# Reordering the hand-over from filter construction to the gated MLP in a one-core S4 + SwiGLU kernel: earlier product of the first block, split additions, weights in other memory

## Chip, cores, metric

The kernel runs on one core of one Trainium2 chip. The metric is the device time of one execution in microseconds (us), the median of several. A span read in a profile runs from the first to the last instruction and is about 1.8 us shorter than the time (310.9 against 312.68 us for the profiled run before).

Engines: PE is the TensorE matmul unit, DVE is VectorE, ACT is ScalarE, POOL is GpSimd. PSUM is the memory that the matmuls here write to.

## The reference

The input x has 2048 tokens of 640 channels. Cut to what matters:

```python
K = einsum("dn,dnl,dn->dl", C, exp(dt*A*l), dt*B).real    # one filter of 2048 taps per channel
u = layernorm(x)
y = causal_fft_convolution(u, K) + u * Dskip              # the kernel does this in blocks of 256 tokens
h = x + y
h2 = h + (silu(ln(h) @ w1) * (ln(h) @ w3)) @ w2           # 640 -> 1536 -> 640
```

## The kernel before

The kernel has two halves. The first builds the filters in the frequency domain, `kf`, for three groups of channels (256, 256 and 128). `k_mm` and `k_dft` are matmuls, `k_evac` and `kf_evac` copy their results out of PSUM. The second half runs eight blocks of 256 tokens, `c` = 0 to 7. For a block, `fwd` is a Fourier transform by matmul, `product` multiplies by `kf` on DVE (block c also needs block c−1), `inv` transforms back, and `h_add` adds the result into the residual and takes its statistics. Then come `ln2_apply`, transposes, six gate/up pairs (`gu`, each ending in a product `hm` on DVE) and two groups of 24 output matmuls (`out_mm`). Four more names: `stats` and `ln1` are the statistics and the scaling of the first layer norm (`ln1` also makes `usd`, the folded input that `fwd` reads), `skip` adds `u * Dskip` into the residual, and `warm` runs matmuls whose result nobody reads, put in for the PE clock. While block c is in its matmuls, DVE and ACT prepare blocks c+1 and c+2.

This is the hand-over, shortened:

```python
    for ig, st in zip(IGS, stg):
        b_mul(2, bt2, "exp", ig, st)          # DVE, last operand for group 2
    warm(6, last_b(2, bt2, 0))
    for b in range(nb[2]):
        pk = k_mm(2, at2, bt2, kc, b)
        k_evac(2, pk, kc, b)
    for q, part in ((0, 0), (0, 1), (1, 0), (1, 1)):
        fwd(0, q, part)
    pb = k_dft(2, kc)
    stats(1); stats(2); skip(0, ulns[0]); ln1(1); skip(1, ulns[1])
    for q, part in ((0, 0), (0, 1)):
        fwd(1, q, part)
    kf_evac(2, pb, "SSVV")                    # kf is complete only here
    # ... (weight loads start, held back until kf is there)
    run(p0, 2)                                # product(0), columns 0-319, all of it behind kf
    for k in range(2): inv_mm(0, k, 0, p1[k])
    run(p0)                                   # columns 320-639
    for k in range(2): inv_mm(0, k, 1, p1[k]); y_evac(0, k, p1[k])
    for q, part in ((1, 0), (1, 1)): fwd(1, q, part)
    h_add(0); r0 = rstd(hst[0][:, :, 1], 2, V)
    # ... (ln2_apply, transposes, their eviction)
```

And the start of the loop over blocks, shortened:

```python
    for c in range(NC):
        pr = product(1) if c == 0 else iter(())
        run(pr, 2)
        for fp in range(FT // 2):             # six gate/up pairs
            gu(c, fp)                         # 10 matmuls each for gate and up, then hm on DVE
            if fp == 0: run(pr); ln1(c + 2)
            if fp in (i0, i0 + 1):
                inv(c + 1, fp - i0)
                if fp == i0 + 1: h_add(c + 1); rs = rstd(...)
            if fp >= 2: fwd(c + 2, (fp - 2) // 2, fp % 2)
            if fp == 3: stats(c + 3)
            if fp == 4 and c: pr = product(c + 2); run(pr, 2)
```

Of the kernel before, what the change touches and what calls it, by code (L numbers as in the profile page):

```python
# [16 lines left out]
II = 16  # L17
# [9 lines left out]
def kernel(  # L27
# [321 lines left out]
    def k_dft(h, kc):  # L349
# [3 lines left out]
        for i in range(II):  # L353
            for f in range(NFT):
# [58 lines left out]

    def bn(mv, k, src):
        st = small.tile([P, 2, V.BN_STATS_DIM], F32, name="st")
        for q in range(2):
            V.bn_stats(out=st[:, q, :], in_=src[:, q * (D // 2):(q + 1) * (D // 2)])  # L417
        V.bn_aggr(out=mv[:, k, :], in_=st[:])
# [30 lines left out]
    def fwd(c, q, part):  # L449
# [4 lines left out]
        pv = ps2()  # L454
# [80 lines left out]
    wts = ctx.enter_context(tc.tile_pool(name="wts", bufs=1, side="right", reuse_waits="tile"))  # L535
    w1sb = wts.tile([P, DT, F], BF16, name="w1sb")
    w3sb = wts.tile([P, DT, F], BF16, name="w3sb")
# [8 lines left out]
    kc = kp.tile([P, II * 4 * 2 * (max(CHUNKS) // 8)], BF16, name="kc")  # L546
    warm(6, last_b(2, bt2, 0))
    for b in range(nb[2]):
        pk = k_mm(2, at2, bt2, kc, b)
        k_evac(2, pk, kc, b)  # L550
    for q, part in ((0, 0), (0, 1), (1, 0), (1, 1)):
        fwd(0, q, part)
    S.activation(out=sil[:], in_=mask[:, 0:1], func=ACT.Silu)
    pb = k_dft(2, kc)
# [5 lines left out]

    def ln1(c):
        ulns[c] = ln1_apply(c, *st1.pop(c), 0)
        fold(c, ulns[c])

    stats(1)
    stats(2)
    skip(0, ulns[0])
    ln1(1)
    skip(1, ulns[1])
    for q, part in ((0, 0), (0, 1)):  # L570
        fwd(1, q, part)
    kf_evac(2, pb, "SSVV")
# [4 lines left out]
    mp = ctx.enter_context(tc.tile_pool(name="mp", bufs=1, side="left", reuse_waits="tile"))  # L577
    w2sb = mp.tile([P, FT, D], BF16, name="w2sb")
# [7 lines left out]
    zz, xx, hst, xls, xts = {}, {}, {}, {}, {}  # L586

    def product(c):


        vt = vts[c]
        t2 = mp.tile([P, 2, 2, D], BF16, name="t2", bufs=1)
        z = mp.tile([P, 2, 2, D], BF16, name="z", bufs=2)
        x = z if c == 0 else mp.tile([P, 2, 2, D], BF16, name="xf", bufs=2)
        zz[c], xx[c] = z, x
        zp = zz.pop(c - 1, None)
        kt = kr if c % 2 else kf
        n = D // 2
        for q in range(2):
            r = slice(q * n, (q + 1) * n)  # L600
            for dst, w in ((z, 0), (t2, 1)):
                kk = mkap(kt[:], w * 2 * D + q * n, [[kt[:].ap[0][0], P], [0, 2], [D, 2], [1, n]])
                V.tensor_tensor(out=dst[:, :, :, r], in0=vt[:, :, :, r], in1=kk, op=ALU.mult)  # L603
            yield
            V.tensor_tensor(out=z[:, 0, :, r], in0=z[:, 0, :, r], in1=t2[:, 1, :, r], op=ALU.subtract)
            V.tensor_tensor(out=z[:, 1, :, r], in0=z[:, 1, :, r], in1=t2[:, 0, :, r], op=ALU.add)
            if c:
                V.tensor_tensor(out=x[:, :, :, r], in0=z[:, :, :, r], in1=zp[:, :, :, r], op=(ALU.add if c % 2 else ALU.subtract))  # L608
            yield

    def inv_mm(c, k, q, py):

        for e in range(2):
            if c % 2:
                lhsT, src = (gn[:, k, :] if e == k else gt[:, 2 * k + e, :]), 1 - k
            else:
                lhsT, src = gt[:, 2 * k + e, :], k
            T.matmul(py[:, q, 0:D // 2], lhsT=lhsT, rhs=xx[c][:, src, e, q * (D // 2):(q + 1) * (D // 2)], start=(e == 0), stop=(e == 1))  # L618

    yss = {}  # L620

    def y_evac(c, k, py):
        if k == 0:
            yss[c] = mp.tile([P, 2, D], BF16, name="ys", bufs=1)
        S.copy(out=yss[c][:, k, :].rearrange("p (q d) -> p q d", q=2), in_=py[:, :, 0:D // 2])

    def h_add(c):
        ys = yss.pop(c)
        yt = mp.tile([P, 2, D], BF16, name="yt", bufs=1)
        V.tensor_tensor(out=yt[:, 0, :], in0=ys[:, 0, :], in1=ys[:, 1, :], op=ALU.add)  # L630
        V.tensor_tensor(out=yt[:, 1, :], in0=ys[:, 0, :], in1=ys[:, 1, :], op=ALU.subtract)
        V.tensor_tensor(out=xs[:, 2 * c:2 * c + 2, :], in0=yt[:], in1=xs[:, 2 * c:2 * c + 2, :], op=ALU.add)  # L632
        hst[c] = small.tile([P, 2, 2], F32, name="hmv")
        for k in range(2):
            bn(hst[c], k, xs[:, 2 * c + k, :])

# [54 lines left out]
    def inv(c, k):  # L691
        py = ps2()
        for q in range(2):
            inv_mm(c, k, q, py)
        y_evac(c, k, py)

    p0, p1 = product(0), [ps2(), ps2()]
    run(p0, 2)
    for k in range(2):
        inv_mm(0, k, 0, p1[k])  # L700
    run(p0)
    for k in range(2):
        inv_mm(0, k, 1, p1[k])
        y_evac(0, k, p1[k])
    for q, part in ((1, 0), (1, 1)):
        fwd(1, q, part)
# [6 lines left out]
    for k in range(2):  # L713
        ln2_apply(0, k, hst[0], r0, k)
        tr_mm(0, k, tp)
    for k in range(2):
        tr_evac(0, k, tp, "SV"[k])

    for c in range(NC):
# [4 lines left out]
        for fp in range(FT // 2):  # L724
            gu(c, fp)
            if fp == 0:
                run(pr)
                if n2:
                    ln1(c + 2)
# [69 lines left out]
```

## Time and profile before

| what | before |
|---|---|
| time, median | 313.11 us in the first five runs, 312.98 over 15 |
| kf complete (last eviction ends) | about 107.2 us |
| first gate matmul | 122.84 us |
| blocks 0 to 6, first gate matmul to the next block's | 27.43, 23.45, 23.06, 23.06, 23.06, 22.37, 21.27 us |

The profile's page gives each engine's busy share in 40 equal slices (a digit is tenths; 9 is 90% or more), and the clock that TensorE was granted:

```profile
PE   3152074645847443988999999999999999999994
...
DVE  6899999999999777669999789789789769462211
...
PEclk9999998576899655899999999999999999999998
```

In slices 3 to 13 DVE is full. From slice 17 on PE is full. Between them, in slices 14 to 16 (101 to 124 us), neither is, and the PE clock is down to about half (digits 6, 5, 5).

Next, the stretch view of the kernel before for that hand-over. The columns are the stretch and its length, then busy us and number of instructions of PE, PE weight loads, DVE, ACT and POOL, then granted clock, DMA share and GB/s:

```profile
94.00:108.00 14.00, 8.41 (x332) 6.10 (x332) 11.38 (x31) 8.50 (x15) 5.78 (x16) 0.84 0.02 4
108.00:118.00 10.00, 3.76 (x12) 1.45 (x12) 7.99 (x19) 5.08 (x8) 0.00 (x0) 0.50 0.97 308
118.00:123.00 5.00, 1.40 (x11) 1.19 (x12) 2.98 (x13) 0.69 (x1) 0.00 (x0) 0.50 1.08 355
```

PE works 5.2 of the 15 us from 108 to 123, at clock 0.50, and DVE leaves 4 of these 15 us empty. Neither engine is full, so this is a chain of waits, and the timeline shows its links. Its columns are start, duration, engine, line, operation, operands, shapes and count, then the idle time before it and what ended it. The DVE and PE lines of the kernel before that matter:

```profile
107.06 0.83 DVE L603 TENSOR_TENSOR z<-vt,kf 128x1280 bf16<-128x1280 bf16 x1 [1.61 <-ACT kf L370]
...
113.65 0.49 DVE L630 TENSOR_TENSOR yt<-ys 128x640 bf16<-128x640 bf16 x1 [1.70 <-ACT ys L625]
...
119.79 0.80 DVE L640 TENSOR_SCALAR xl<-xs,hmv,rs 128x640 bf16<-128x640 bf16 x2
...
122.30 0.49 DVE L654 COPY xt<-ps 128x640 bf16<-128x640 bf16 x1 [1.71 <-ACT xt L652]
...
122.84 2.29 PE L665 MATMUL ps<-xt,w1sb 128*128 128x256 bf16 x10 [1.31 <-DVE xt L654]
...
128.47 0.43 DVE L673 TENSOR_TENSOR hm<-sg,up 128x512 bf16<-128x512 bf16 x1 [2.43 <-ACT up L672]
...
133.45 0.43 PE L457 MATMUL ps<-usd,ft 128*128 128x320 bf16 x2 [0.81 <-DVE usd L446]
```

The product waits for the last `kf` eviction until 107.06, and the residual addition for the evicted inverse until 113.65. The layer norm starts at 119.79, the first gate matmul at 122.84. Even then DVE waits 2.43 us for the first gate/up result before the rest of `product(1)` and `ln1(2)`, which makes PE wait 0.81 us for block 2's folded input `usd` at 133.45.

All waits of PE after 118 us in the kernel before (who waited for whom, us in total, times, longest):

```profile
PE ps L645 <- DVE xl L640: 5.9, 1, 5.9
PE ps L679 <- DVE hm L673: 3.7, 5, 1.4
PE ps L665 <- DVE xt L654: 1.3, 1, 1.3
PE ps L457 <- DVE usd L446: 0.8, 1, 0.8
PE ps L618 <- DVE xf L608: 0.2, 1, 0.2
```

Inside the blocks the only repeated one is the output matmul on the last `hm`, five times. The timeline of block 3 shows how it arises:

```profile
200.27 0.42 DVE L673 TENSOR_TENSOR hm<-sg,up 128x512 bf16<-128x512 bf16 x1 [1.55 <-ACT up L672]
...
203.00 0.43 DVE L673 TENSOR_TENSOR hm<-sg,up 128x512 bf16<-128x512 bf16 x1 [0.66 <-ACT up L672]
...
214.99 0.42 DVE L673 TENSOR_TENSOR hm<-sg,up 128x512 bf16<-128x512 bf16 x1
...
215.47 0.72 PE L679 MATMUL ps<-w2sb,hm 128*128 128x320 bf16 x4 [0.53 <-DVE hm L673]
```

DVE has two holes early in the block (1.55 and 0.66 us, both waits for an evicted gate/up pair). The last `hm` starts at 214.99, and PE waits 0.53 us for that.

### The profile page before, as it was taken

The numbers are of one execution on the slowest core, as the hardware profiler recorded it, in microseconds if no ns is written. First come the engines' busy times: TensorE is split into PE (matmuls) and PEld (weight loads), VectorE is DVE, ScalarE is ACT, GpSimd is POOL, SyncE is SP. The second block draws the span as 40 slices with busy tenths as digits, with TensorE's granted clock in tenths as the row PEclk, the third lists the DMA queues.
The fourth block names the chain that finished last, engine by engine and source line by source line (L and its number), as shares of the span: only waits on it lengthen the run. The fifth ranks groups of instructions, "written<-read, shape, count | busy, mean of one in ns | idle before, by whom it ended". The sixth has DMA issues, their size and how long they took to land.

```text
span 310.9 us, 6842 instructions
## 1 busy us (share of the span) xinstructions
PE 234.5 (75%) x2770; PEld 185.0 (60%) x2770; DVE 246.8 (79%) x543; ACT 191.4 (62%) x389; POOL 45.2 (15%) x137
## 2 busy tenths in 40 slices
PE   3152074645847443988999999999999999999994
PEld 1121043543634212776886887887887887887882
DVE  6899999999999777669999789789789769462211
ACT  3999999999937452364465465465465465544441
POOL 4022000000003300005315015015015020020000
PEclk9999998576899655899999999999999999999998
DMA  6731910000000099200000100100100100100001
GB/s 185 211 154 34 236 36 0 2 2 3 2 3 2 7 332 354 73 2 0 24 21 0 44 2 1 44 0 3 42 2 0 44 0 2 42 2 21 24 1 43
DMA packets 12018, 15.58 MB, mean 50 GB/s; under 512 B 2002, under 2 KB 11346, under 8 KB 11858
## 3 DMA queue, kind: packets, MB, share of 16 engines
q1 hardware_dynamic: 11426, 14.95, 15.6%
q8 instruction: 21, 0.34, 0.5%
q10 hardware_dynamic: 560, 0.20, 0.3%
q14 instruction: 11, 0.09, 0.1%
HBM read 12.26 MB, written 2.88 MB: 49 GB/s over the span
## 4 chain that ended last, share of the span: by engine, by line
DVE 52%; PE 37%; ACT 6%; issue 3%; POOL 0%; DVEq 0%; POOLq 0%; ACTq 0%
PE ps L665 19%; PE ps L679 11%; DVE at L307 6%; DVE st L417 6%; DVE tt L309 6%; DVE at L312 6%; DVE bt L283 3%; DVE bt L282 3%; DVE hm L673 2%; DVE t L603 2%; DVE z L603 2%; DVE xf L608 2%; DVE xs L632 2%; PE ps L645 1%; PE ps L618 1%
## 5 line engine op out<-in xcount | busy, mean ns | idle before, releaser
L665 PE MATMUL ps<-xt,w1sb 128*128 128x256 bf16 x480 | 61.5, 276 | 1.3 <-DVE xt L654 1.3
L670 ACT ACTIVATE sg<-ps 128x512 bf16<-128x512 f32 x48 | 28.7, 597 | 54.4 <-PE ps L665 54.4
L665 PE MATMUL ps<-xt,w3sb 128*128 128x256 bf16 x480 | 61.3, 276 | 0.0
L679 PE MATMUL ps<-w2sb,hm 128*128 128x320 bf16 x384 | 55.5, 299 | 3.7 <-DVE hm L673 3.7
L665 PEld LDWEIGHTS <-w1sb 128*128 128x128 bf16 x480 | 47.6, 99 | 9.4 <-issue 1.5
L665 PEld LDWEIGHTS <-w3sb 128*128 128x128 bf16 x480 | 47.5, 99 | 5.9
L679 PEld LDWEIGHTS <-hm 128*128 128x128 bf16 x384 | 36.8, 98 | 19.1 <-DVE hm L673 5.6
L673 DVE TENSOR_TENSOR hm<-sg,up 128x512 bf16<-128x512 bf16 x48 | 19.6, 422 | 33.6 <-ACT up L672 33.6
L408 POOL TENSOR_TENSOR ta<-rs 128x2 f32<-128x2 f32 x30 | 8.6, 286 | 188.7 <-DVE rs L406 187.6
L687 ACT CAST ob<-ps 128x640 bf16<-128x640 f32 x16 | 11.1, 692 | 36.3 <-PE ps L679 36.3
L417 DVE BATCH_NORM_STATS2 st<-xs 128x6 f32<-128x320 bf16 x64 | 27.4, 471 | 2.4 <-DMA xs<-in_A_u_dram 2.1
L672 ACT CAST up<-ps 128x512 bf16<-128x512 f32 x48 | 27.8, 579 | 0.0
L325 PE MATMUL ps<-bt,at 128*128 128x128 bf16 (+1 forms) x320 | 19.9, 247 | 8.7 <-ACT kc L345 7.8
L325 PEld LDWEIGHTS <-at 128*128 128x128 bf16 (+1 forms) x320 | 17.2, 110 | 12.4 <-issue 9.3
L458 ACT CAST vt<-ps 128x640 bf16<-128x640 f32 x32 | 22.2, 706 | 3.2 <-PE ps L457 3.2
L253 ACT ACTIVATE bt<-alp 128x384 bf16<-128x384 f32 (+1 forms) x45 | 20.8, 461 | 0.0
L307 DVE TENSOR_TENSOR at<-at,zs 128x1536 bf16<-128x1536 bf16 (+3 forms) x30 | 20.3, 677 | 0.0
L309 DVE TENSOR_TENSOR tt<-at,zs 128x1536 bf16<-128x1536 bf16 (+3 forms) x30 | 20.3, 675 | 0.0
L312 DVE TENSOR_TENSOR at<-at,tt 128x1536 bf16<-128x1536 bf16 (+3 forms) x30 | 19.1, 678 | 0.5
L379 PEld LDWEIGHTS <-ident 128*128 128x128 bf16 x36 | 4.2, 123 | 22.2 <-issue 17.2
L358 PE MATMUL ps<-kc,wt 32*128 32x64 bf16 (+1 forms) x768 | 8.5, 202 | 11.7 <-ACT kc L345 6.3
L457 PE MATMUL ps<-usd,ft 128*128 128x320 bf16 x64 | 14.7, 318 | 2.5 <-ACT kc L345 1.0
(116 smaller groups left out, 379.1 us busy)
## 6 DMA issues: line engine op xcount, KB each, us to landing
xs<-in_A_u_dram SPq DMA_DIRECT2D x4, 640.0 KB, 5.1
out_dram<-ot SPq DMA_DIRECT2D x16, 160.0 KB, 1.8
wt<-ftd SPq DMA_DIRECT2D x4, 512.0 KB, 7.5
w1sb<-in_B_w_dram SPq DMA_DIRECT2D x3, 640.0 KB, 6.9
w3sb<-in_B_w_dram SPq DMA_DIRECT2D x3, 640.0 KB, 9.5
w2sb<-in_B_w_dram SPq DMA_DIRECT2D x1, 1920.0 KB, 14.5
ftd<-fl SPq DMA_DIRECT2D x1, 256.0 KB, 2.1
par_ar<-in_A_A_re_dram SPq DMA_DIRECT2D x2, 96.0 KB, 3.9
```

The source lines that it names most:

```text
L253: S.activation(out=dst, in_=grp(h, 1), func=ACT.Sin, scale=-float(i))
L307: V.tensor_tensor(out=av[:, part, :, o0:o0 + w, :], in0=src, in1=z4[:, 0].broadcast_to([P, cw // 2, w, 2]), op=ALU.mult)
L309: V.tensor_tensor(out=tv[:, part], in0=src, in1=z4[:, 1].broadcast_to([P, cw // 2, w, 2]), op=ALU.mult)
L312: V.tensor_tensor(out=dst, in0=dst, in1=tv[:, 1 - part], op=(ALU.add if part else ALU.subtract))
L325: T.matmul(pk[:, half, gi * P:(gi + 1) * P], lhsT=at[r, c], rhs=bt[r, c], start=first, stop=last, tile_position=((r.start, 0) if n1 else N ...
L417: V.bn_stats(out=st[:, q, :], in_=src[:, q * (D // 2):(q + 1) * (D // 2)])
L458: S.copy(out=vts[c][:, part, :, r], in_=pv[:, :, 0:D // 2])
L665: T.matmul(pg[:, b, u * TB:(u + 1) * TB], lhsT=w[:, kt, fb * P:(fb + 1) * P], rhs=xts[c][:, kt, :], start=(kt == 0), stop=(kt == DT - 1))
L670: S.activation(out=sg[:], in_=pg[:, 0, :], func=ACT.Silu)
L672: S.copy(out=up[:], in_=pg[:, 1, :])
L673: V.tensor_tensor(out=hms[c][:, 2 * fp:2 * fp + 2, :].rearrange("p u t -> p (u t)"), in0=sg[:], in1=up[:], op=ALU.mult)
L679: T.matmul(po[:, q, 0:D // 2], lhsT=hms[c][:, fb, k * P:(k + 1) * P], rhs=w2sb[:, fb, q * (D // 2):(q + 1) * (D // 2)], start=(fb == 0), s ...
```

## The change

The intent is to take work out of the chain behind the last `kf` eviction. Columns 0 to 511 belong to filter groups 0 and 1 and are complete long before group 2. So their product, inverse and residual addition go ahead of it, the inverse into the middle of `k_dft(2)`. Only 128 columns are left behind. For that `fwd(0)` moves ahead of `k_mm(2)`. `fwd(1)` and `skip(1)` move behind the residual addition of block 0, and the second half of `product(1)` and `ln1(2)` move ahead of block 0's first `hm`. `h_add` is split by column halves in every block. The two first weight matrices move into memory that becomes free later. The core of the diff:

```diff
-    def k_dft(h, kc):
+    def k_dft(h, kc, mid=None):
         for i in range(II):
+            if mid and i == II // 2:
+                mid()
+    HALVES = [slice(0, D // 2), slice(D // 2, D)]
+    SPLIT = [slice(0, d0s[-1]), slice(d0s[-1], D)]        # 512 and 128 columns
@@ fwd
-        pv = ps2()
+        pv = ps2("g" if c == 0 and q != part else "d")
@@ hand-over
-    warm(6, last_b(2, bt2, 0))
+    for q, part in ((0, 0), (0, 1), (1, 0), (1, 1)):
+        fwd(0, q, part)
+    skip(0, ulns[0])
+    stats(1)
+    warm(2, last_b(2, bt2, 0))
+    p0 = product(0, SPLIT)
     for b in range(nb[2]):
         pk = k_mm(2, at2, bt2, kc, b)
+        if b:
+            run(p0, 2)
         k_evac(2, pk, kc, b)
-    pb = k_dft(2, kc)
-    stats(1) ; stats(2) ; skip(0) ; ln1(1) ; skip(1) ; half of fwd(1)       (shortened)
-    kf_evac(2, pb, "SSVV")
+    pb = k_dft(2, kc, lambda: inv(0, SPLIT[0]))
+    stats(2)
+    h_add(0, SPLIT[0])
+    kf_evac(2, pb, "SSSS")
+    run(p0)
+    ln1(1)
+    inv(0, SPLIT[1])
     ... (kr)
+    warm(8, xs[:, 12:14, 0:256].rearrange("p a (b c) -> p a b c", b=1))
+    h_add(0, SPLIT[1])
+    h_stats(0)
     ... (rstd, ln2_apply, transposes)
+    skip(1, ulns[1])
     ... (eviction of the transposes)
+    for q, part in ((0, 0), (0, 1), (1, 0), (1, 1)):
+        fwd(1, q, part)
@@ loop over blocks
+            if c == 0 and fp == 0:
+                run(pr)
+                ln1(2)
             gu(c, fp)
             if fp == 0:
                 run(pr)
-                if n2:
+                if n2 and c:
                     ln1(c + 2)
             if n1 and fp in (i0, i0 + 1):
-                inv(c + 1, fp - i0)
+                inv(c + 1, HALVES[fp - i0])
+                h_add(c + 1, HALVES[fp - i0])
                 if fp == i0 + 1:
-                    h_add(c + 1)
+                    h_stats(c + 1)
```

More of the change, by code (lines that the diff above doesn't have):

```diff
@@ L412, in rstd @@
         return rs
+    HALVES = [slice(0, D // 2), slice(D // 2, D)]
+    SPLIT = [slice(0, d0s[-1]), slice(d0s[-1], D)]
     def bn(mv, k, src):
         st = small.tile([P, 2, V.BN_STATS_DIM], F32, name="st")
-        for q in range(2):
-            V.bn_stats(out=st[:, q, :], in_=src[:, q * (D // 2):(q + 1) * (D // 2)])
+        for q, r in enumerate(HALVES):
+            V.bn_stats(out=st[:, q, :], in_=src[:, r])
         V.bn_aggr(out=mv[:, k, :], in_=st[:])
@@ L534 @@
     bctx.close()
-    wts = ctx.enter_context(tc.tile_pool(name="wts", bufs=1, side="right", reuse_waits="tile"))
-    w1sb = wts.tile([P, DT, F], BF16, name="w1sb")
-    w3sb = wts.tile([P, DT, F], BF16, name="w3sb")
     vp = ctx.enter_context(tc.tile_pool(name="vp", bufs=4, side="right", reuse_waits="tile"))
@@ L545 @@
         b_mul(2, bt2, "exp", ig, st)
-    kc = kp.tile([P, II * 4 * 2 * (max(CHUNKS) // 8)], BF16, name="kc")
-    warm(6, last_b(2, bt2, 0))
-    for b in range(nb[2]):
-        pk = k_mm(2, at2, bt2, kc, b)
-        k_evac(2, pk, kc, b)
     for q, part in ((0, 0), (0, 1), (1, 0), (1, 1)):
         fwd(0, q, part)
-    S.activation(out=sil[:], in_=mask[:, 0:1], func=ACT.Silu)
-    pb = k_dft(2, kc)
     st1 = {}
@@ L559, in stats, with product @@
         st1[c] = (mv, rstd(mv[:, :, 1][:, 0:2], 2, G))
+    skip(0, ulns[0])
+    stats(1)
+    kc = kp.tile([P, II * 4 * 2 * (max(CHUNKS) // 8)], BF16, name="kc")
+    warm(2, last_b(2, bt2, 0))
+    zz, xx, hst, hpart, xls, xts = {}, {}, {}, {}, {}, {}
+    def product(c, cuts=HALVES):
+        vt = vts[c]
+        t2 = vp.tile([P, 2, 2, D], BF16, name="t2", bufs=1)
+        z = vp.tile([P, 2, 2, D], BF16, name="z", bufs=2)
+        x = z if c == 0 else vp.tile([P, 2, 2, D], BF16, name="xf", bufs=2)
+        zz[c], xx[c] = z, x
+        zp = zz.pop(c - 1, None)
+        kt = kr if c % 2 else kf
+        for r in cuts:
+            for dst, w in ((z, 0), (t2, 1)):
+                kk = mkap(kt[:], w * 2 * D + r.start, [[kt[:].ap[0][0], P], [0, 2], [D, 2], [1, r.stop - r.start]])
+                V.tensor_tensor(out=dst[:, :, :, r], in0=vt[:, :, :, r], in1=kk, op=ALU.mult)
+            yield
+            V.tensor_tensor(out=z[:, 0, :, r], in0=z[:, 0, :, r], in1=t2[:, 1, :, r], op=ALU.subtract)
+            V.tensor_tensor(out=z[:, 1, :, r], in0=z[:, 1, :, r], in1=t2[:, 0, :, r], op=ALU.add)
+            if c:
+                V.tensor_tensor(out=x[:, :, :, r], in0=z[:, :, :, r], in1=zp[:, :, :, r], op=(ALU.add if c % 2 else ALU.subtract))
+            yield
@@ new lines, with inv @@
+    yss = {}
+    def inv(c, r):
+        py, n = ps2(), r.stop - r.start
+        for k in range(2):
+            for e in range(2):
+                if c % 2:
+                    lhsT, src = (gn[:, k, :] if e == k else gt[:, 2 * k + e, :]), 1 - k
+                else:
+                    lhsT, src = gt[:, 2 * k + e, :], k
+                T.matmul(py[:, k, 0:n], lhsT=lhsT, rhs=xx[c][:, src, e, r], start=(e == 0), stop=(e == 1))
+        if r.start == 0:
+            yss[c] = vp.tile([P, 2, D], BF16, name="ys", bufs=1)
+        S.copy(out=yss[c][:, :, r], in_=py[:, :, 0:n])
@@ new lines, in h_add @@
+    def h_add(c, r):
+        ys = yss[c]
+        if r.start == 0:
+            hpart[c] = vp.tile([P, 2, D], BF16, name="yt", bufs=1), small.tile([P, 2, 2, V.BN_STATS_DIM], F32, name="hst")
+        yt, st = hpart[c]
+        V.tensor_tensor(out=yt[:, 0, r], in0=ys[:, 0, r], in1=ys[:, 1, r], op=ALU.add)
+        V.tensor_tensor(out=yt[:, 1, r], in0=ys[:, 0, r], in1=ys[:, 1, r], op=ALU.subtract)
+        V.tensor_tensor(out=xs[:, 2 * c:2 * c + 2, r], in0=yt[:, :, r], in1=xs[:, 2 * c:2 * c + 2, r], op=ALU.add)
+        for k in range(2):
+            V.bn_stats(out=st[:, k, int(r.start > 0), :], in_=xs[:, 2 * c + k, r])
@@ L561, in ln1, with h_stats @@
+    def h_stats(c):
+        hst[c] = small.tile([P, 2, 2], F32, name="hmv")
+        for k in range(2):
+            V.bn_aggr(out=hst[c][:, k, :], in_=hpart[c][1][:, k])
     def ln1(c):
@@ L563, in ln1 @@
         fold(c, ulns[c])
-    stats(1)
-    stats(2)
-    skip(0, ulns[0])
-    ln1(1)
-    skip(1, ulns[1])
-    for q, part in ((0, 0), (0, 1)):
-        fwd(1, q, part)
-    kf_evac(2, pb, "SSVV")
+    p0 = product(0, SPLIT)
+    for b in range(nb[2]):
+        pk = k_mm(2, at2, bt2, kc, b)
+        if b:
+            run(p0, 2)
+        k_evac(2, pk, kc, b)
+    S.activation(out=sil[:], in_=mask[:, 0:1], func=ACT.Silu)
+    pb = k_dft(2, kc, lambda: inv(0, SPLIT[0]))
+    stats(2)
+    h_add(0, SPLIT[0])
+    kf_evac(2, pb, "SSSS")
     kctx.close()
@@ L577 @@
     mp = ctx.enter_context(tc.tile_pool(name="mp", bufs=1, side="left", reuse_waits="tile"))
+    w1sb = mp.tile([P, DT, F], BF16, name="w1sb")
+    w3sb = mp.tile([P, DT, F], BF16, name="w3sb")
     w2sb = mp.tile([P, FT, D], BF16, name="w2sb")
@@ L585 @@
     nc.sync.dma_start(out=w2sb[:], in_=B_w2.rearrange("(s p) d -> p s d", p=P))
-    zz, xx, hst, xls, xts = {}, {}, {}, {}, {}
-    def product(c):
-        vt = vts[c]
-        t2 = mp.tile([P, 2, 2, D], BF16, name="t2", bufs=1)
-        z = mp.tile([P, 2, 2, D], BF16, name="z", bufs=2)
-        x = z if c == 0 else mp.tile([P, 2, 2, D], BF16, name="xf", bufs=2)
-        zz[c], xx[c] = z, x
-        zp = zz.pop(c - 1, None)
-        kt = kr if c % 2 else kf
-        n = D // 2
-        for q in range(2):
-            r = slice(q * n, (q + 1) * n)
-            for dst, w in ((z, 0), (t2, 1)):
-                kk = mkap(kt[:], w * 2 * D + q * n, [[kt[:].ap[0][0], P], [0, 2], [D, 2], [1, n]])
-                V.tensor_tensor(out=dst[:, :, :, r], in0=vt[:, :, :, r], in1=kk, op=ALU.mult)
-            yield
-            V.tensor_tensor(out=z[:, 0, :, r], in0=z[:, 0, :, r], in1=t2[:, 1, :, r], op=ALU.subtract)
-            V.tensor_tensor(out=z[:, 1, :, r], in0=z[:, 1, :, r], in1=t2[:, 0, :, r], op=ALU.add)
-            if c:
-                V.tensor_tensor(out=x[:, :, :, r], in0=z[:, :, :, r], in1=zp[:, :, :, r], op=(ALU.add if c % 2 else ALU.subtract))
-            yield
-    def inv_mm(c, k, q, py):
-        for e in range(2):
-            if c % 2:
-                lhsT, src = (gn[:, k, :] if e == k else gt[:, 2 * k + e, :]), 1 - k
-            else:
-                lhsT, src = gt[:, 2 * k + e, :], k
-            T.matmul(py[:, q, 0:D // 2], lhsT=lhsT, rhs=xx[c][:, src, e, q * (D // 2):(q + 1) * (D // 2)], start=(e == 0), stop=(e == 1))
-    yss = {}
-    def y_evac(c, k, py):
-        if k == 0:
-            yss[c] = mp.tile([P, 2, D], BF16, name="ys", bufs=1)
-        S.copy(out=yss[c][:, k, :].rearrange("p (q d) -> p q d", q=2), in_=py[:, :, 0:D // 2])
-    def h_add(c):
-        ys = yss.pop(c)
-        yt = mp.tile([P, 2, D], BF16, name="yt", bufs=1)
-        V.tensor_tensor(out=yt[:, 0, :], in0=ys[:, 0, :], in1=ys[:, 1, :], op=ALU.add)
-        V.tensor_tensor(out=yt[:, 1, :], in0=ys[:, 0, :], in1=ys[:, 1, :], op=ALU.subtract)
-        V.tensor_tensor(out=xs[:, 2 * c:2 * c + 2, :], in0=yt[:], in1=xs[:, 2 * c:2 * c + 2, :], op=ALU.add)
-        hst[c] = small.tile([P, 2, 2], F32, name="hmv")
-        for k in range(2):
-            bn(hst[c], k, xs[:, 2 * c + k, :])
     def ln2_apply(c, k, mv, rs, kr):
@@ L689, in out_add @@
         nc.sync.dma_start(out=out[:, tt, :], in_=ot[:])
-    def inv(c, k):
-        py = ps2()
-        for q in range(2):
-            inv_mm(c, k, q, py)
-        y_evac(c, k, py)
-    p0, p1 = product(0), [ps2(), ps2()]
-    run(p0, 2)
-    for k in range(2):
-        inv_mm(0, k, 0, p1[k])
-    run(p0)
-    for k in range(2):
-        inv_mm(0, k, 1, p1[k])
-        y_evac(0, k, p1[k])
-    for q, part in ((1, 0), (1, 1)):
-        fwd(1, q, part)
+    run(p0)
+    ln1(1)
+    inv(0, SPLIT[1])
     for part in range(2):
@@ L709 @@
             S.mul(out=kr[:, part, e, :], in_=kf[:, 1 - part, e, :], mul=(1.0 if part == e else -1.0))
-    h_add(0)
+    warm(8, xs[:, 12:14, 0:256].rearrange("p a (b c) -> p a b c", b=1))
+    h_add(0, SPLIT[1])
+    h_stats(0)
     r0 = rstd(hst[0][:, :, 1], 2, V)
-    tp = ps2("d", BF16)
+    tp = ps2("g", BF16)
     for k in range(2):
@@ L738 @@
                 stats(c + 3)
-            if fp == 4:
-                if n2 and c:
-                    pr = product(c + 2)
-                    run(pr, 2)
+            if n2 and c and fp == 4:
+                pr = product(c + 2)
+                run(pr, 2)
         po = out_mm(c, 0)
```

## The prediction

> **What bounds the kernel now.** Three regimes, by the timeline and the stretch table of the trace before.
> 1. Until 107 us VectorE is the limit (17.8 of 18 us busy in 76–94).
> 2. From 94 to 123 us a latency chain fills the pipeline (chain of waits): last b_mul 94.2, k_mm(2), kc evictions to 99.1, four fwd(0) evictions, k_dft(2) 100.7–104.9 (1.8 us of it "issue"), last kf eviction 107.1 behind two fwd(1) evictions, all of product(0) and its inverse to 113.6, h_add(0), statistics and rstd to 119.8, ln2, transposes, first gate matmul at 122.84. In 108–123 PE is busy 5.2 of 15 us. VectorE idles about 8 us between 104 and 128.5.
> 3. From 122.84 PE is the limit. Blocks c=0..7 take 27.4, 23.6, 23.1, 23.1, 23.1, 22.4, 21.3, 19.7 us. Block 0 carries about 2 us of half clock and waits of 1.4 us (out matmul on hm), 0.8 us (fwd on usd) and 0.2 us; blocks 1–4 wait 0.75, 0.53, 0.53, 0.53 us on the last hm.
>
> **What the change moves.** fwd(0) goes into the hole before k_mm(2). Columns 0–511 of product(0), their inverse (inside k_dft(2)) and h_add run before the last kf eviction; only 128 columns stay behind it. fwd(1), skip(1), product(1) move behind h_add(0); every h_add is split and starts after the first gate/up pair. Weight tiles move to memory freed later, but their DMA was already gated by kf.
>
> **Cost.** VectorE bf16 multiplies issue 0.73 us apart for 1280 elements; by estimate 2048 elements cost 1.13 us, 512 cost 0.33.
> - k_mm(2) waits for the last fwd(0) eviction: about 96.8 instead of 94.4; k_dft(2) starts near 101.6 (was 100.7) and holds the 1.0–1.3 us inverse; kf ready at about 107, as before.
> - VectorE ends: skip(0) 95.9, stats(1) 98.5, product S0 102, stats(2) 104.7, h_add S0 107.7, small product 108.8, ln1(1) 110.4, small h_add and statistics 112, rstd 114.2, ln2 115.7, skip(1) 117.3, xt eviction 117.9. Gate matmul at about 118.5: 4.3 us earlier.
> - product(1) and ln1(2) are done near 126.5 (were 133.7), so block 0 loses its late usd and hm waits: about 2 us. Half clock at its start stays.
> - The split h_add fills VectorE idle time (1.55 and 0.66 us early in block 3) for 0.25 us of added overhead, so the last hm is ready about 1 us earlier: about 0.5 us in each of blocks 1–4, 2 us in all.
>
> Sum: 4.3 + 2 + 2 = 8.3 us, nearly all on the chain: **305.0 us**; range **302.0 to 309.0**. Chances: faster 0.72, same 0.26, slower 0.02.
>
> **What would show it.** First gate matmul at 117–120 us; kf complete within 1 us of 107; block 0 near 25 us; blocks 2–4 near 22.5 us without the out matmul's wait on hm; VectorE idle between 95 and 126 under 3 us; weights landed before use (the first 0.64 MB lands in 6.9 us now).
>
> **What would make it wrong.** [...] granted clock 0.50 from about 103, back near 127.3. The hole before k_mm(2) is now sparser: a cold k_mm could cost 3 us. Conversely the eight warm-up matmuls may let block 0 start at full clock, 2 us better. Product S0 later than 103 would stall k_dft(2).

The sum came to 4.3 + 2 + 2 = 8.3 us. The sizes can be worked out from the trace before. DVE multiplies of 640 and 1280 elements issue 0.41 and 0.73 us apart (101.91 and 122.71 us), which gives about 1.12 us for 2048 elements and 0.34 for 512; two halves cost 0.09 us more than one whole, about 0.26 us for the three additions of `h_add`. `k_mm(2)` took 3.16 us at clock 1.00 (94.43), and ten gate or up matmuls were 2.09 us apart at 0.50 (122.84 to 124.93) and 1.09 us at 1.00 (128.35 to 129.44), so half clock could cost `k_mm(2)` about 2.9 us.

## More of the kernel before

The timelines show an engine's instructions in the order of the statements (DVE in the kernel before: product of block 0 at 107.06, its residual addition at 113.65, layer norm at 119.79, first `hm` at 128.47 us).

## The result

The time is 303.04 us (median of 8 runs, 302.58 to 303.95) against 312.98 us over 15. The ratio is 0.9683, with a 95% interval from 0.9671 to 0.9695: 3.2% faster. A ratio here is always the mean time of one kernel's fast runs over that of the other's fast runs of the same rounds, so it is not quite the ratio of the medians quoted. The profiled spans differ by 8.7 us (310.9 and 302.2).

| what | before | after | difference |
|---|---|---|---|
| first gate matmul, us | 122.84 | 118.20 | −4.64 |
| block 0 | 27.43 | 23.73 | −3.70 |
| block 1 | 23.45 | 23.68 | +0.23 |
| blocks 2, 3, 4 | 23.06 each | 22.88, 22.89, 22.88 | −0.53 in all |
| blocks 5 and 6 | 22.37, 21.27 | 22.38, 21.26 | 0 |

The sum is −8.64 us, which accounts for the span. The same three lines of the page, after:

```profile
PE   2243055544767658999998999999999999999994
...
DVE  7799999999999998889999789789789769732111
...
PEclk9999999557977965999999999999999999999999
```

The stretch view after, same columns:

```profile
94.00:108.00 14.00, 8.86 (x329) 6.19 (x327) 13.52 (x32) 8.89 (x17) 6.53 (x16) 0.87 0.02 4
108.00:118.00 10.00, 7.22 (x30) 3.54 (x31) 8.52 (x31) 4.92 (x9) 0.00 (x0) 0.50 1.04 327
118.00:123.00 5.00, 5.00 (x34) 3.82 (x33) 4.90 (x9) 2.12 (x4) 0.00 (x0) 0.70 1.08 356
```

DVE is now busy 13.5 of 14 us in the first stretch (11.4 before) and 4.9 of 5 in the last (3.0 before). PE is full from 118 us on.

The timeline of the changed kernel, for the links of the chain:

```profile
101.21 1.19 PE L360 MATMUL ps<-kc,wt 32*128 32x32 bf16 x128 [1.55 <-ACT kc L345]
...
102.33 1.04 PE L594 MATMUL ps<-z,gt 128*128 128x512 bf16 x4
...
105.77 0.77 ACT L372 CAST kf<-ps 128x128 bf16<-128x128 f32 x4 [1.30 <-PE ps L360]
...
107.41 0.41 DVE L575 TENSOR_TENSOR z<-vt,kf 128x512 bf16<-128x512 bf16 x1
...
110.24 0.22 DVE L605 TENSOR_TENSOR yt<-ys 128x128 bf16<-128x128 bf16 x1
...
113.99 0.80 DVE L649 TENSOR_SCALAR xl<-xs,hmv,rs 128x640 bf16<-128x640 bf16 x2
...
118.20 2.34 PE L674 MATMUL ps<-xt,w1sb 128*128 128x256 bf16 x10
...
125.86 0.76 DVE L682 TENSOR_TENSOR hm<-sg,up 128x512 bf16<-128x512 bf16 x2
```

The inverse of 512 columns (102.33) sits inside `k_dft(2)`. `kf` is complete at 106.54. The small product starts at 107.41, the small addition at 110.24, the layer norm at 113.99, 5.8 us earlier than before. The first gate matmul is at 118.20, and the first `hm` at 125.86 already has all of `product(1)` and `ln1(2)` behind it.

The same question for the waits of PE after 118 us. Two of the five kinds before belonged to the hand-over, which here lies mostly ahead of 118 us (the transposes wait 1.94 us for the layer norm until 114.50). The three kinds inside the blocks have become one:

```profile
PE ps L688 <- DVE hm L682: 2.2, 4, 1.2
```

One of these four waits is 1.16 us long, in block 1. The other three are 0.36 us, one in each of blocks 2 to 4. Block 3, DVE first, then the output matmul on PE:

```profile
191.98 0.42 DVE L682 TENSOR_TENSOR hm<-sg,up 128x512 bf16<-128x512 bf16 x1 [1.55 <-ACT up L681]
...
193.96 0.32 DVE L605 TENSOR_TENSOR yt<-ys 128x320 bf16<-128x320 bf16 x1
...
199.89 0.43 DVE L682 TENSOR_TENSOR hm<-sg,up 128x512 bf16<-128x512 bf16 x1 [0.50 <-ACT up L681]
...
202.86 0.42 DVE L682 TENSOR_TENSOR hm<-sg,up 128x512 bf16<-128x512 bf16 x1
203.20 0.82 DVE L575 TENSOR_TENSOR z<-vt,kr 128x1280 bf16<-128x1280 bf16 x1
...
206.53 0.42 DVE L682 TENSOR_TENSOR hm<-sg,up 128x512 bf16<-128x512 bf16 x1
```

```profile
207.00 0.72 PE L688 MATMUL ps<-w2sb,hm 128*128 128x320 bf16 x4 [0.36 <-DVE hm L682]
```

The hole of 1.55 us before the block's first `hm` is still there. A new hole of 0.50 us stands before the fourth `hm`, and the last `hm` is late again.

### The profile page after: what moved, and what is told of

Its sections match the earlier page's. It is cut to its first block, busy times and chain, and to the rows that moved or that the text cites. A ratio compares the mean times of both kernels' runs of the same rounds, so it can differ in the third digit from the quotient of the medians.

```text
span 302.2 us, 6878 instructions
## 1 busy us (share of the span) xinstructions
PE 235.6 (78%) x2774; PEld 186.0 (62%) x2774; DVE 248.4 (82%) x565; ACT 191.6 (63%) x391; POOL 46.2 (15%) x137
## 4 chain that ended last, share of the span: by engine, by line
DVE 50%; PE 42%; ACT 4%; issue 2%; POOL 0%; DVEq 0%; POOLq 0%
PE ps L674 25%; PE ps L688 12%; DVE at L307 6%; DVE tt L309 6%; DVE at L312 6%; DVE st L422 4%; DVE bt L283 3%; DVE bt L282 3%; DVE t L575 2%; PE ps L594 2%; DVE z L575 2%; DVE hm L682 2%; DVE xf L580 2%; PE ps L654 2%; DVE hst L609 1%
## 5 line engine op out<-in xcount | busy, mean ns | idle before, releaser
L674 PE MATMUL ps<-xt,w3sb 128*128 128x256 bf16 x480 | 60.6, 273 | 0.0
L325 PE MATMUL ps<-bt,at 128*128 128x128 bf16 (+1 forms) x320 | 19.1, 240 | 9.1 <-ACT kc L345 9.0
L381 PEld LDWEIGHTS <-ident 128*128 128x128 bf16 x40 | 5.1, 134 | 23.4 <-issue 19.1
L360 PE MATMUL ps<-kc,wt 32*128 32x64 bf16 (+1 forms) x768 | 9.8, 214 | 12.0 <-ACT kc L345 7.9
L360 PEld LDWEIGHTS <-wt 32*128 32x128 bf16 x768 | 9.2, 112 | 13.1 <-issue 12.9
L697 DVE TENSOR_TENSOR ot<-ob,xs 128x640 bf16<-128x640 bf16 x16 | 7.8, 487 | 10.3 <-ACT ob L696 10.3
```

The costliest lines, as they stand in the source:

```text
L325: T.matmul(pk[:, half, gi * P:(gi + 1) * P], lhsT=at[r, c], rhs=bt[r, c], start=first, stop=last, tile_position=((r.start, 0) if n1 else N ...
L360: T.matmul(ob.rearrange("p (h b x) -> p b h x", h=2, x=8), lhsT=wt[32 * blk:32 * blk + 32, i, f * P:(f + 1) * P], rhs=rb.rearrange("p (b h ...
L674: T.matmul(pg[:, b, u * TB:(u + 1) * TB], lhsT=w[:, kt, fb * P:(fb + 1) * P], rhs=xts[c][:, kt, :], start=(kt == 0), stop=(kt == DT - 1))
```

## The experiments

The theory had three parts. First, the earlier work on 512 columns shortens the chain behind `kf`. Second, block 0 gains because DVE is ahead when it starts. Third, the split `h_add` fills DVE's holes in every block. The rivals were the move of `fwd(0)` alone, the eight warm-up matmuls (PE clock), and, for the late `hm`, the order of DVE's work late in the block. Twelve runs were made, all correct: eleven other kernels, and the changed one once more as a control. This table has first gate matmuls and block times (us) from the profiles; the last column is the time, with the ratio to the kernel before:

| kernel | first gate matmul | block 0 | block 1 | block 3 | time, ratio |
|---|---|---|---|---|---|
| before | 122.84 | 27.43 | 23.45 | 23.06 | 312.98 |
| changed | 118.20 | 23.73 | 23.68 | 22.89 | 303.04, 0.9683 |
| changed, control | 117.68 | 22.82 | 23.67 | 22.89 | 302.97, 0.9671 |
| whole_product | 123.81 | 22.66 | 23.64 | 22.88 | 308.10, 0.9835 |
| early_fwd0 | 123.63 | 27.41 | 23.44 | 23.05 | 313.27, 1.0001 |
| old_block0 | 118.09 | 25.04 | 23.67 | 22.89 | 304.06, 0.9705 |
| whole_hadd | 118.10 | 25.01 | 23.31 | 22.88 | 304.45, 0.9715 |
| no_warm8 | 118.14 | 22.69 | 23.68 | 22.89 | 302.98, 0.9676 |
| warm13 | 117.50 | 22.87 | 23.66 | 22.89 | 302.51, 0.9665 |
| ln1_first | 118.10 | 23.53 | 23.68 | 22.89 | 303.27, 0.9683 |
| stats_early | 117.72 | 23.14 | 23.68 | 22.37 | 301.28, 0.9623 |
| stats_defer | 117.48 | 22.86 | 22.37 | 22.38 | 304.62, 0.9702 |
| early_warm13 | 117.51 | 22.87 | 23.69 | 22.37 | 301.09, 0.9612 |
| ln2_on_act | 117.48 | 23.25 | 22.59 | 22.37 | 300.28, 0.9581 |

The runs were made in three sets, and only the set of no_warm8, warm13 and ln1_first has the changed kernel itself beside it (the control). Across sets, compare the ratios: by them whole_product, whole_hadd and old_block0 are 4.8, 1.0 and 0.7 us above the changed kernel, where the times say 5.1, 1.4 and 1.0.

### whole_product: the product of block 0 back behind kf

```diff
-    SPLIT = [slice(0, d0s[-1]), slice(d0s[-1], D)]
+    SPLIT = HALVES
-        if b:
-            run(p0, 2)
-    pb = k_dft(2, kc, lambda: inv(0, SPLIT[0]))
-    h_add(0, SPLIT[0])
+    pb = k_dft(2, kc)
+    run(p0, 2)
+    inv(0, SPLIT[0])
     run(p0)
+    h_add(0, SPLIT[0])
     h_add(0, SPLIT[1])
```

> Changed kernel with all 640 columns of product(0), its inverse and h_add(0) put back behind the last kf eviction (all else, also the early fwd(0), late fwd(1), warm-up matmuls and split h_add, stays). Theory (work of 512 columns moved ahead of kf is what shortens the fill): first gate matmul 3.5 to 4.5 us later than in the changed kernel (about 122), total about 306.5 to 307.5 us. Rival (the early fwd(0), the late fwd(1) and the shorter way of kf do it): first gate matmul within 1 us of 118.2, total under 304.3.

It took 308.10 us (interval of the ratio 0.9814 to 0.9856), 5 us above the changed kernel and a little above the range. The DVE timeline of this run shows where it went:

```profile
106.72 0.83 DVE L575 TENSOR_TENSOR z<-vt,kf 128x1280 bf16<-128x1280 bf16 x1 [5.59 <-ACT kf L372]
```

DVE stands idle for 5.59 us until `kf` is there. The residual addition starts at 113.16, where the changed kernel starts its small one at 110.24, and must do all 640 columns. The gate matmuls start 5.6 us later than in the changed kernel:

```profile
123.81 1.56 PE L671 MATMUL ps<-xt,w1sb 128*128 128x256 bf16 x10
```

So moving 512 columns ahead of `kf` is worth about 5 us, and the first part of the theory holds. Everything else of the change is still in this kernel (early `fwd(0)`, late `fwd(1)`, the memory of the weights), so none of it brings the gate matmuls forward by itself. The run shows a second thing: block 0 stays short (22.66 us) though the chain is as long as before. Block 0's gain therefore does not come from the shorter chain.

### early_fwd0: only fwd(0) moved, on the kernel before

```diff
         b_mul(2, bt2, "exp", ig, st)
+    for q, part in ((0, 0), (0, 1), (1, 0), (1, 1)):
+        fwd(0, q, part)
     ...
-    for q, part in ((0, 0), (0, 1), (1, 0), (1, 1)):
-        fwd(0, q, part)
```

(The two PSUM tags of the change are in as well.)

> Kernel before with only fwd(0) moved ahead of k_mm(2), with the two PSUM tags of the change. Theory: k_mm(2) starts 1.5 us later, k_dft(2) about as before, first gate matmul within 1 us of 122.84, total 312 to 314 us. Rival (early fwd(0) alone opens the way for kf): over 2 us faster, 311 us or less.

It took 313.27 us, ratio 1.0001 (0.9982 to 1.0020). Moving `fwd(0)` is worth nothing by itself. It is only what makes the early product possible.

### old_block0: the old DVE order in block 0 only

```diff
-            if c == 0 and fp == 0:
-                run(pr)
-                ln1(2)
             gu(c, fp)
             if fp == 0:
                 run(pr)
-                if n2 and c:
+                if n2:
                     ln1(c + 2)
```

> Changed kernel with the old VectorE order in block 0 alone: second half of product(1) and ln1(2) again behind the first hm. Theory (block 0 gained because VectorE no longer waits for the first hm and so has usd(2) and later hm in time): VectorE idles about 2 us before the first hm, fwd(2) waits on usd(2) 0.8 to 1.5 us and the out matmul of block 0 waits up to 1 us again, total 1 to 2.5 us above the changed kernel, 304 to 305.5. Rival (the earlier start of VectorE's work before block 0 is enough by itself): within 0.5 us of 303.0.

It took 304.06 us (0.9684 to 0.9726), 1.0 us above the changed kernel. The two intervals overlap. The DVE timeline shows the hole, and the PE waits show its price:

```profile
122.90 0.43 DVE L682 TENSOR_TENSOR hm<-sg,up 128x512 bf16<-128x512 bf16 x1 [1.97 <-ACT up L681]
```

```profile
PE ps L462 <- DVE usd L451: 1.3, 1, 1.3
```

DVE waits 1.97 us for the first gate/up pair with `product(1)` half done, and PE then waits 1.3 us on `usd`. Block 0 takes 25.04 us for 23.73, with about as long at half clock (2.6 and 2.8 us). This is the prediction's late `usd`, made and unmade by one reordering. The out matmul's expected extra wait in block 0 did not come.

### whole_hadd: h_add in one piece again

```diff
-                h_add(c + 1, HALVES[fp - i0])
                 if fp == i0 + 1:
+                    h_add_whole(c + 1)
                     h_stats(c + 1)
```

> Changed kernel with h_add of blocks 1 to 7 in one piece again behind the second inverse (the inverse and its eviction still by column halves). From the trace after (blocks 2 to 4 are 0.17 us shorter each than before, the last hm still 0.36 us late): 0.3 to 1.0 us slower than the changed kernel, about 303.3 to 304. The prediction's own step (0.5 us a block in four blocks): 2 us slower, about 305.

It took 304.45 us (0.9690 to 0.9739), 1.4 us above the changed kernel, more than the expected range and less than the prediction's step. The loss is in block 0 (25.01 for 23.73), where the output matmuls wait for the last `hm` again, 1.18 us (138.20); block 1 gives 0.37 us back. So block 0 needs both the new order and the split: without either it takes 25.0 us. All waits on `hm` in this run:

```profile
PE ps L700 <- DVE hm L694: 3.0, 5, 1.2
```

Blocks 2 to 4 are as short as with the split (22.88 us). DVE in block 3 of this run, the third and fourth, then the last `hm`:

```profile
200.34 0.79 DVE L694 TENSOR_TENSOR hm<-sg,up 128x512 bf16<-128x512 bf16 x2
...
207.34 0.42 DVE L694 TENSOR_TENSOR hm<-sg,up 128x512 bf16<-128x512 bf16 x1
```

With the whole `h_add` DVE reaches the third and fourth `hm` together at 200.34, just when the fourth gate/up pair has been evicted, and the last `hm` starts 7.00 us later: 0.36 us for the third `hm` and 6.64 us from the fourth on. With the split DVE is there 0.50 us too early, waits, and again the last `hm` starts 6.64 us after the fourth. Both end equally late. So in the steady blocks the split gained nothing. The 0.17 us a block against the kernel before must have another source. A guess is `h_stats`: this kernel too issues the two aggregations side by side at the end, and its `h_add` with statistics takes 4.22 us (196.12 to 200.34) where the kernel before took 4.44 (203.59 to 208.03). That was not run by itself, so it is not shown.

### after_again and no_warm8: the control, and the eight warm-up matmuls

> The changed kernel itself, as the control on this chip for the three runs beside it: about 303.0 us, ratio to the kernel before 0.968; granted clock back at full 2 to 5 us after the first gate matmul.

The control gave 302.97 us, ratio 0.9671 (0.9653 to 0.9689). The clock was back 0.94 us after the first gate matmul, earlier than the 2 to 5 us expected.

```diff
-    warm(8, xs[:, 12:14, 0:256].rearrange("p a (b c) -> p a b c", b=1))
```

> Changed kernel without the eight warm-up matmuls between the second inverse of block 0 and the transposes. Theory A (they let block 0 recover the clock earlier): half clock for about 4.5 us after the first gate matmul as in the kernel before, 1 to 2 us slower than the changed kernel. Theory B, from the trace after (clock falls at 107.35 and returns at 121.0[...]): same within 0.6 us.

Without them the time is 302.98 us, ratio 0.9676 (0.9657 to 0.9696): the same as the control. Theory A falls. The granted clock was read in steps of 0.25 us from 88 to 132 us in eleven profiles: outside of the steps with a change in them it was 0.50 or 1.00. In the profiled run of the kernel before it fell at 103.55 and returned at 127.45. In the changed kernel it fell at 107.4 and returned at 121.0, and the warm-up matmuls (108.94 to 112.56) lay wholly in between. In the control, the same kernel, it returned at 111.8 while they ran (108.87 to 112.21), fell again at 115.2 (PE was busy for 1.14 us from 111.80 to 115.15), and was back for good at 118.6. In the run without them it fell at 101.8 and was back at 118.8. So the half clock ended at 121.0 and 118.6 us with them and at 118.8 without them: they don't decide it. In all three it ended during the first gate matmuls, behind `fwd(1)`. That the unbroken work of these two ends it is the author's estimate; what decides the time was not shown. The clock is also behind the 23.73 and 22.82 us that the same kernel needed for block 0 in two profiles: half clock lasted 2.80 us into the block in one and 0.94 us in the other. In the five profiles in which PE waits for nothing inside block 0 and the clock was read (changed, control, whole_product, no_warm8, ln1_first), block 0 less half of its time at half clock comes to 22.33 to 22.36 us.

### warm13: thirteen instead of eight

```diff
-    warm(8, ...)
+    warm(13, ...)
```

> Changed kernel with thirteen warm-up matmuls in place of eight, 5.5 us that end about where the transposes begin (114.5). Theory B: [...] the clock returns near 114.2, transposes take 0.7 us for 1.25 and block 0 runs at full clock from its start: 1.0 to 2.0 us faster than the changed kernel, about 301 to 302. Rival (the clock follows the gate matmuls only): same within 0.4 us. If they run into the transposes: up to 0.5 us slower.

It took 302.51 us, ratio 0.9665 (0.9647 to 0.9684). The clock did what Theory B said, back at 114.4 (the thirteen ran from 108.91 to 114.58), and PE's timeline shows the transposes in 0.81 us for 1.25 and full rate from the first gate matmul (1.25 us for ten, 2.34 in the profile after):

```profile
114.45 0.81 PE L654 MATMUL ps<-ident,xl 128*128 128x128 bf16 x10
...
117.50 1.25 PE L674 MATMUL ps<-xt,w1sb 128*128 128x256 bf16 x10
```

The time is 0.5 us under the control, with intervals that overlap, and not the 1 us expected at least. PE now waits 0.35 us on `usd(2)`, because it has caught up with DVE, and the control itself was partly at full clock. The spans say more than the times: all five runs have spans of 300.6 or 300.7 us, the control's four 300.7 to 301.3. So the gain is about 0.5 us at the median, and the scatter of the span is gone.

### ln1_first: fill the hole before the first hm

```diff
-            if c == 0 and fp == 0:
-                run(pr)
-                ln1(2)
-            gu(c, fp)
             if fp == 0:
                 run(pr)
-                if n2 and c:
+                if n2:
                     ln1(c + 2)
+            gu(c, fp)
```

> Changed kernel with ln1(c+2) of blocks 1 to 5 put ahead of the block's first hm, as the change does for block 0 alone. Theory (the 1.55 us that VectorE idles in each block lies before the first hm, where the split h_add cannot reach; ln1 can): VectorE is about 1.5 us earlier in blocks 2 to 4, the wait of the out matmul on the last hm (0.36 us each) goes, block 1 (VectorE never idle there, wait 1.16 us) hardly changes: 0.8 to 1.5 us faster than the changed kernel, about 301.5 to 302.2. Rival (the wait comes from the order late in the block, not from VectorE being late): same within 0.3 us.

It took 303.27 us, ratio 0.9683 (0.9664 to 0.9702): no gain, so my theory fell and the rival stood. DVE in block 3 of this run:

```profile
191.76 0.42 DVE L682 TENSOR_TENSOR hm<-sg,up 128x512 bf16<-128x512 bf16 x1
...
199.59 0.43 DVE L682 TENSOR_TENSOR hm<-sg,up 128x512 bf16<-128x512 bf16 x1 [1.40 <-ACT up L681]
...
206.23 0.42 DVE L682 TENSOR_TENSOR hm<-sg,up 128x512 bf16<-128x512 bf16 x1
```

The hole before the first `hm` is gone (191.76, nothing ahead of it), but it has come back before the fourth: 1.40 us. From the fourth `hm` to the start of the last one DVE works 6.64 us without a hole, as in the profile after: `hm`, `stats` (2.63 us with its gaps), `hm`, half a product (3.33 us). The fourth `hm` can't start before its gate/up pair is evicted, so the last `hm` comes at a fixed distance from PE's own work. Whatever is saved earlier turns into waiting there.

### stats_early: shorten that run of work

```diff
-            if n3 and fp == 3:
+            if n3 and fp == (2 if c else 3):
                 stats(c + 3)
```

(This is on top of ln1_first.)

> ln1_first, and stats(c+3) of blocks 1 to 4 put one gate/up pair earlier (behind the second half of h_add, ahead of the fourth hm). From the trace of ln1_first: VectorE's last idle time before the late hm is 1.40 us ahead of the fourth hm, and from there stats 2.63, hm 0.34, product half 3.33, hm 0.34 us run without a hole, so the last hm comes 0.36 us late whatever was gained earlier. Theory (this run of work is the limit): with stats moved ahead of the hole the last hm of blocks 2 to 4 comes in time, these blocks take about 22.5 us for 22.88, block 1 stays near 23.7 (VectorE has no hole there): 0.8 to 1.3 us faster than the changed kernel, 301.7 to 302.2. Rival (PE's 22.88 has another cause): blocks stay at 22.88.

It took 301.28 us, ratio 0.9623 (0.9594 to 0.9652), a little better than the range. Blocks 2 to 4 take 22.37 us, which is what block 5 takes in every kernel, having no `stats`. In the same block DVE now has 0.88 us to spare before the fifth `hm`, and the last one comes in time:

```profile
200.77 0.42 DVE L682 TENSOR_TENSOR hm<-sg,up 128x512 bf16<-128x512 bf16 x1 [0.88 <-ACT up L681]
...
204.44 0.42 DVE L682 TENSOR_TENSOR hm<-sg,up 128x512 bf16<-128x512 bf16 x1
```

The fixed run from a late `hm` to the last one was the limit of blocks 2 to 4, and this is shown. The 0.88 us is also the first sign of slack that the output matmul does not pay for.

### stats_defer: take work out of block 1

```diff
-            if n3 and fp == (2 if c else 3):
+            if n3 and c != 1 and fp == (2 if c else 3):
                 stats(c + 3)
     ...
         po = out_mm(c, 1)
         out_add(c, 1, po)
+        if c == 1:
+            stats(4)
```

(This is on top of stats_early and warm13.)

> stats_early with thirteen warm-up matmuls, and stats(4) of block 1 put at the end of block 1, behind the last hm. Theory (block 1 is bound by VectorE's total work since the middle of block 0, 1.16 us too much before the last hm; block 2 has holes that can take the 2.6 us): block 1 falls to 22.5 to 22.8 us, block 2 is at most 22.9, blocks 3 and 4 at 22.5: 2.0 to 3.0 us faster than the changed kernel, 300.0 to 301.0. If block 2 can not absorb it: block 2 above 23.2 and no more than 1.5 us in all.

It took 304.62 us, worse than the changed kernel. Block 1 fell to 22.37 us as expected, so block 1 is indeed held up by DVE's total work. But block 2 rose to 27.37 us. The deferred statistics end in a chain of eight tiny operations on POOL, which `ln1(4)`, now ahead of the first `hm`, has to await:

```profile
169.54 0.80 DVE L435 TENSOR_SCALAR uln<-xs,mv,rs 128x640 bf16<-128x640 bf16 x2 [2.24 <-POOL rs L413]
```

That chain takes about 2.1 us of latency (167.38 to 169.5 in this trace), and with `stats(5)` in the same block DVE was 2.52 us late for the last `hm`. In the profiled run more was lost behind that wait: the granted clock was 0.50 from 185.3 to 188.7 us, and the next 24 output matmuls took 5.10 us where they take 3.42 at full clock. Two of the six runs have spans of 301.1 us in place of 302.7 to 302.9; they may be runs without this fall of the clock (the 3.4 us at half clock cost an estimated 1.7 us, 5.10 less 3.42), but neither was profiled. The work was moved to a place where its latency counted.

### early_warm13 and ln2_on_act: a version better than both

```diff
-    warm(8, ...)
+    warm(13, ...)
```

(This is on top of stats_early.)

> stats_early with thirteen warm-up matmuls for eight. The two gains lie in different stretches (blocks 2 to 4; clock at the start of block 0) and should add: 0.2 to 0.8 us under stats_early (301.3), so 300.5 to 301.1, block 0 near 22.8 at full clock from its start in every run, so that the runs scatter less.

stats_early with thirteen warm-up matmuls took 301.09 us, ratio 0.9612 (0.9585 to 0.9639), 0.2 us under stats_early and inside its interval. The two may add, but this does not prove it. Its block 0 was 22.87 us. One of the six times is 302.01 us, but the span of that run is 299.1 us, so its excess lies outside the span. The six spans are 299.0 to 299.3 us, where those of stats_early are 299.2 to 301.4: the scatter of the span went, as expected.

The second gives the scaling of the second layer norm to ACT, from block 1 on. That takes 0.72 us a block off DVE (two instructions, from 161.09 to the next one at 161.81 in the trace after):

```diff
+        if c:
+            S.activation(out=xls[c][:, k, :], in_=xs[:, 2 * c + k, :], func=ACT.Identity,
+                         scale=rs[:, kr:kr + 1], bias=nbs[c][:, k:k + 1])
+            return
         V.tensor_scalar(out=xls[c][:, k, :], ...)
     ...
                     rs = rstd(hst[c + 1][:, :, 1], 2, G)
+                    nbs[c + 1] = small.tile([P, 2], F32, name="nb")
+                    G.tensor_tensor(out=nbs[c + 1][:], in0=hst[c + 1][:, :, 0], in1=rs[:, 0:2], op=ALU.mult)
+                    G.tensor_scalar(out=nbs[c + 1][:], in0=nbs[c + 1][:], scalar1=-1.0, scalar2=None, op0=ALU.mult)
```

> early_warm13 with the scaling of ln2[...] on ScalarE for blocks 1 to 7, its bias from two small GpSimd operations. Theory (block 1 waits 1.16 us on the last hm because VectorE works without a hole from the middle of block 0; any 1.2 us less does it, and no wait comes in its place, unlike in stats_defer): block 1 falls from 23.7 to 22.4 us, 1.0 to 1.4 us faster than early_warm13, about 299.3 to 300. If ScalarE or GpSimd then sets the pace (bias late, transposes wait): block 0 or others grow by 0.5 us or more and the gain is lost.

It took 300.28 us (300.07 to 300.42), ratio 0.9581 (0.9555 to 0.9606). No wait of an output matmul on `hm` is left. Block 1 fell from 23.69 to 22.59 us. Block 0 rose by 0.38 us (transposes wait 0.21 us for the ACT result there), so 0.8 us of the expected 1.0 to 1.4 arrived, about what came off DVE. In early_warm13 the output matmuls waited 1.16 us for the last `hm` of block 1 (until 159.70); the 0.72 us off DVE and the 0.38 us of the longer block 0 come to 1.10 of that, by an estimate from these numbers. This is the best version, 4.2% faster than the kernel before by the ratio.

## Why the prediction was right

The time was predicted at 305.0 us with a range of 302.0 to 309.0; 303.04 lies inside, and the 3.2% is on the side given 0.72.

- **First gate matmul at about 118.5: right.** It was 118.20. The links matched: `k_dft(2)` at 101.21 (101.6 predicted), `kf` at 106.54 (107), small addition and statistics over at 111.7 (112), ln2 from 113.99 (from 114.2). The run whole_product shows the cause: without the early columns the start is back at 123.81.
- **The estimates of DVE cost: right.** 2048 elements issued 1.14 us apart (98.45 to 99.59 in the trace; 1.13 predicted), 512 elements 0.32 us apart (0.33). The record of one instruction of 2048 elements is 1.22 us long.
- **"About 2 us" in block 0: right mechanism, too small.** It was 3.70 us in the profile. The waits that the term named were 1.38, 0.81 and 0.15 us in the trace before, 2.34 in all, and all of them went. Set beside each other by PE's timeline, the first two gate/up pairs gave 0.86 us (half clock for 2.8 us for 4.6), the other pairs with the `usd` wait 1.28, the output matmuls and transposes 1.56. The prediction had said "Half clock at its start stays". It stayed, but shorter, and not the same twice: 2.80 us in this profile and 0.94 us in the control, which gained another 0.9 us. That part was luck. Nor is this split by stage one by cause: in early_fwd0 half clock lasted 5.4 us into block 0, and the block took the same 27.4 us as in the kernel before, so with the old DVE order the waits on DVE swallow such a difference. The alternative it named, that the eight warm-up matmuls might bring full clock, is not what happened: no_warm8 is as fast. The feared stall of `k_dft(2)` by a late early product did not come (it was done at 102.13, and the prediction had set the limit at 103). The cold `k_mm` came in part: the clock was at half from 93.7 to 97.1 us, and `k_mm(2)` took 3.70 us for 3.16.
- **"About 0.5 us in each of blocks 1–4, 2 us in all": this step failed.** Measured: +0.23 us in block 1 and −0.17 or −0.18 us in blocks 2, 3 and 4, so 0.3 us in all. The prediction counted the hole of 1.55 us as one that the split could fill, but that hole lies ahead of the block's first `hm`, and `h_add` comes behind it on DVE. And time gained early in a block is lost again before the fourth `hm`, which waits for PE and ACT; from there to the last `hm` 6.64 us of work follow without a hole. ln1_first (the hole filled, no gain) and stats_early (that run of work shortened, waits gone) show it. whole_hadd shows that the split brought nothing to blocks 2 to 4; it helps block 0, by about 1.3 us. In block 1 DVE is full from the middle of block 0 on, with one wait of 0.17 us from 131.1 to 165.6 in the trace after, as stats_defer and ln2_on_act confirm from two sides; block 0 got shorter and left its work to block 1, whose wait on `hm` grew from 0.75 to 1.16 us.
- **Weights: right.** Their loads start at 107.1, and no gate matmul waits for one in either trace. Moving them was not run by itself.

In the profile the sum is 8.64 us against 8.3 predicted: block 0 gave 1.7 us more than its term and the start 0.3 us more, the steady blocks 1.7 us less. That the last two cancel is luck: one term was mis-sized and another failed. The time fell further, by 9.9 us between the medians, because the profiled run of the changed kernel (303.95 us) was the slowest of its eight, 0.9 us above their median, and that of the kernel before 0.3 us below its own. The runs of the changed kernel lie between 302.58 and 303.95 us. The time at half clock moved block 0 by 0.9 us between two profiles, so it can account for much of that scatter; this is not shown, as only one of the eight runs has a profile.

## What to carry to other kernels

When one late input holds up a whole stage, look for the part of the stage that doesn't need it (here four fifths of the columns), and pay for it in the hole that the waiting leaves. A hole in an engine's time could be filled here only by work that stood, in that engine's order, ahead of what ended the hole; and before counting on a fill, follow the engine to the next instruction that waits for another engine, because time gained ahead of such a meeting point is given back there. To shorten a repeated late arrival, shorten the run of work between the last meeting point and the late result.

## What the traces leave open

- When the clock falls. It fell after 3.41 us in which PE was busy for 1.73 us (kernel before, 100.09 to 103.50), after 1.67 of 3.40 us (changed kernel, 90.30 to 93.70) and after 1.14 of 3.35 us (control, 111.80 to 115.15). It stayed at full after 1.61 and 1.66 of 3.40 us (kernel before, 83.1 to 86.5 and 89.9 to 93.3). So busy time over such stretches does not tell when.
- When it returns. It was still at half after 2.80 of 3.41 us (changed kernel, 114.19 to 117.60) and returned after 3.41 of 3.41 (117.60 to 121.01). Eight warm-up matmuls were worth nothing (no_warm8), though in the control the clock was back from 111.8 to 115.2. With thirteen it was at full in the first gate matmuls in each of the four profiles that have them (warm13, stats_defer, early_warm13, ln2_on_act): the first ten took 1.25 us. These busy times use modelled matmul ends.
- In `k_dft(2)`, 256 small matmuls with their weight loads at about 9 ns each (128 in 1.19 us), PE stopped with nothing to wait for that the profile shows ("issue"): for 1.77 us in the kernel before, 1.07 us in the changed kernel, 2.20 us in whole_product, and not at all in the control. What it does in that time was not tried.
